# The bank of a gate product: from the transposes' pool of two to the w_in product's pool of three

## The chip, the cores and the metric
One core of a Trainium2 chip runs the program. The metric is the device time of one execution in microseconds (us), as a median over runs. The profile is one more execution, seen through the hardware profiler.

## What is computed
Two batches of 768 tokens go through three stages. The second and third are cut here to what matters:

```python
attn_out = _attn_ref(q, k, v)                 # linear attention with decay, 8 heads of 64
x = attn_out.transpose(0, 2, 1, 3).reshape(B, S, H * D)      # (2, 768, 512)
h = np.maximum(x @ w_in, 0.0)                 # w_in 512 x 1024
gate = 1 / (1 + np.exp(-conv3(h, conv_w)))    # over neighbouring tokens
x = (h * gate) @ w_out                        # w_out 1024 x 512
logits = x @ w_gate                           # 8 experts, and w_local beside it
h = np.maximum(x[b, s] @ w1[e], 0.0)          # e: the token's expert
out[b, s] = p[e] * (h @ w2[e])
```

The kernel doesn't wait for `x` to have the logits: it forms `w_out @ [w_gate, w_local]` (1024 x 9) once and multiplies it by `h * gate`.

## The kernel before
The order of instructions on each engine is the order in which the program's Python issues them; a scheduler only adds the waits. Several generators are advanced by hand, so that their steps interleave.

**The attention** goes over 48 chunks (8 pairs of heads, 6 chunks of 128 tokens). PSUM has eight banks: one for the gate's logits (`psl`), five for the attention (`ps1`: two for `s_ps`, one for `inc`, two for `y`), one for the conversions (`psg`), one for the w_in product (`psa`).

**The w_in product** of a batch is done in 8 blocks of 128 of the 1024 hidden columns (`ffn_in`). A block has two halves, a and b, of 384 tokens; each half is one PSUM tile `h_ps`, filled by four *slices* (k = 0 to 3) of three matmuls each (L133 to L135), and then evicted by ScalarE (L364). I count the slices of the first batch from 0, eight a block: slices 0 to 19 are issued in the attention's shadow, slice 20 (the second half of block 2) is the first behind it. `tick()` runs after each slice and issues the next step of the blocks already multiplied: L338 (ScalarE), L341 twice (VectorE), L343 (sigmoid, ScalarE), L345 (VectorE), L314 (ScalarE), L318 (VectorE), and in the end the gate's logits (`logit`, L332, TensorE), which need the block's gate weights `wc[:, m]`.

**The conversions** (`convert`) bring the weights, which come as 64-bit words, to two fp32 parts. A conversion loads its words (`raw`), narrows them (L149 and L150 VectorE, L151 ScalarE, L153 GpSimd, into a tile `na`), writes the high part (L171 ScalarE) and the low part (L173). For a block m of w_out it goes on: TensorE transposes the block (*turn m*, L182, tile `wt_ps`), ScalarE copies it to SBUF (L186, tile `wt` in the pool of `na`), TensorE multiplies it by the gate's weights (*product m*, L190, tile `wc_ps`, 9 columns), and ScalarE copies those into `wc` (*gate copy m*, L192). `advance()` moves all running conversions by one step, once per chunk and behind the attention once per slice. The list `turning` holds back a turn while as many blocks as `banks` has entries are between turn and gate copy.

Behind the attention the pools are made anew: `psa` has three banks, for `h_ps`, `psg` two and `psb` two (the w_out product's), and `banks` gets its second entry. Blocks 0 and 1 of w_out have then been turned, and product 1 is the first to be issued; seven products (1 to 7) and six turns (2 to 7) are left. In the kernel before both `wt_ps` and `wc_ps` come from `psg`:

```python
        ps = psg.tile([P, 4, P], F32, tag="g", name="wt_ps")     # L180, the turn's
        pg = psg.tile([P, E + 1], F32, tag="g", name="wc_ps")    # the product's
```

A new tile waits for the last reader of the tile that had its bank. Both kinds are read by ScalarE alone, and so is `h_ps`.

After that: the second batch's w_in product, the w_out product and the routing (L474 to L642), and then the experts (11 tiles of tokens and 2 of quarters), for which SyncE fetches weights in 152 transfers of 512 KB.

Of the kernel before, what the change touches and what calls it, by code (L numbers as in the profile page):

```python
# [9 lines left out]
F32 = mybir.dt.float32  # L10
# [11 lines left out]
E, F = 8, 1024  # L22
NT = B * S
P = 128
# [67 lines left out]
def tile_kernel(ctx, tc, cat, cst, qT, kT, kN, vN, w_in, conv_w, w_out, wg, w1, w2, out):  # L92
# [4 lines left out]
    def pool(name, bufs, stack=ctx, **kw):  # L97
        return stack.enter_context(tc.tile_pool(name=name, bufs=bufs, reuse_waits="tile", **kw))
# [17 lines left out]
    psg = pool("psg", 1, ps_stack, space=PSUM)  # L116
    psa = pool("psa", 1, ps_stack, space=PSUM)
# [23 lines left out]
    def raw_words(src, n):  # L141
        r = p1.tile([P, 512, 2], I32, tag="raw", name="raw", bufs=3)
        sy.dma_start(out=r[:, 0:n].rearrange("p n t -> p (n t)"), in_=src.bitcast(I32))
        return r[:, 0:n, 0], r[:, 0:n, 1]

    def narrow(words, n):
        lo, hi = words
        a = p1.tile([P, 512], I32, tag="na", name="na", bufs=4)[:, 0:n]
        ve.tensor_scalar(out=a, in0=hi, scalar1=3, scalar2=0x3FFFFFF8, op0=ALU.logical_shift_left, op1=ALU.bitwise_and)  # L149
        ve.scalar_tensor_tensor(out=a, in0=hi, scalar=-0x40000000, in1=a, op0=ALU.bitwise_and, op1=ALU.bitwise_or)  # L150
        se.activation(out=lo, in_=lo.bitcast(U32), func=AF.Copy, scale=2.0 ** -29)  # L151
        yield 2
        po.tensor_tensor(out=a, in0=a, in1=lo, op=ALU.add)  # L153
        yield 2
        return a.bitcast(F32)

    turning, held, loaded, ready, banks = [], [], [], [], [0]

    def convert(src, hi, lo, m=None):

        while len(loaded) > 2:
            yield 1
        loaded.append(src)
        words = raw_words(src, 512)
        yield 6
        while len(held) > 2:
            yield 1
        held.append(src)
        w = yield from narrow(words, 512)
        loaded.pop()  # L170
        se.activation(out=hi, in_=w, func=AF.Copy)  # L171
        yield 2
        (po if m is None else ve).tensor_tensor(out=lo, in0=w, in1=hi.bitcast(F32), op=ALU.subtract)  # L173
        if m is None:
            held.pop()
            return
        while len(turning) >= len(banks):
            yield 1
        turning.append(m)
        ps = psg.tile([P, 4, P], F32, tag="g", name="wt_ps")  # L180
        for k in range(4):
            te.transpose(ps[:, k, :], w[:, k * P:(k + 1) * P], ident)  # L182
        held.pop()
        yield 2
        wt = p1.tile([P, 512], F32, tag="na", name="wt", bufs=4).rearrange("p (k n) -> p k n", k=4)
        se.activation(out=wt, in_=ps, func=AF.Copy)  # L186
        yield 2 if len(banks) == 1 else 7
        pg = psg.tile([P, E + 1], F32, tag="g", name="wc_ps")
        for k in range(4):
            te.matmul(pg, wt[:, k, :], wgs[:, k, :], start=(k == 0), stop=(k == 3))  # L190
        yield 1
        se.activation(out=wc[:, m, 0:E + 1], in_=pg, func=AF.Copy)  # L192
        turning.remove(m)
        ready.append(m)
# [220 lines left out]
    for i in range(len(seq) + LOOK):  # L415
        if i < len(seq):
            p, c = seq[i]
            heads[p].scores(c)
            if c == 0 and p + 1 < 8:
                running.append([heads[p + 1].prepare(), 2])  # L420
            if i in STARTS:
                running.append([convert(*parts.pop(0)), 1])
            if i in LOADS:
                load(LOADS[i])
            if i == 14:
                running.append([small(), 1])
        todo = rest
        if i >= LOOK:
            p, c = seq[i - LOOK]
            rest = heads[p].output(c)  # L430
        if todo:
            todo()
        advance()
        while i >= FIRST and slices < (i - FIRST + 1) * RATE:
            next(first)
            slices += 1
# [6 lines left out]
    psa = pool("psa", 3, q_stack, space=PSUM)  # L443
    psg = pool("psg", 2, q_stack, space=PSUM)
# [330 lines left out]
    psa = pool("psc", 1, space=PSUM)  # L775
# [270 lines left out]
```

## Time and profile before
| | us |
|---|---|
| median of 3 runs | 443.0 |
| lowest, highest run | 442.42, 445.74 |
| the profiled execution | 441.8 |
| its span, first to last instruction | 440.0 |
| TensorE busy in it | 409.7 (93%) |
| VectorE, ScalarE, GpSimd busy | 289.3, 260.0, 91.7 |

The mean granted clock of TensorE is 0.984 of its full speed. All times that follow are from the start of the span. In the rows of the order of time a busy TensorE is modelled at its ends, so the start of the next instruction often lies before the end of the one ahead; distances are therefore taken from start to start where there are two.

### The profile page before, as it was taken

Reading aid. Unit: us, or ns where it says so; the run is one execution under the profiler, and the core shown is the slowest. Engines: PE = TensorE matmul, PEld = TensorE weight load, DVE = VectorE, ACT = ScalarE, POOL = GpSimd, SP = SyncE. Lnnn points to the kernel's source line nnn. Section 1 sums busy time; section 2 is a strip of 40 time slices with the busy share of each in tenths; the row PEclk is TensorE's granted clock in tenths of the full one; section 3 lists DMA queues with packets and bytes.
Section 4 is the critical chain, followed back from the end, with each engine's and each line's share of the span. In section 5 each row is a group of like instructions: output and inputs, shape, how many; then the busy total and the mean of one; then the engine's idle time right before and its main releaser. Section 6 shows DMA issues by size and latency. Waiting matters only on the chain.

```text
span 440.0 us, 7232 instructions
## 1 busy us (share of the span) xinstructions
PE 409.7 (93%) x2378; PEld 324.6 (74%) x2378; DVE 289.3 (66%) x517; ACT 260.0 (59%) x429; POOL 91.7 (21%) x93
## 2 busy tenths in 40 slices
PE   4988999986999999999899999999999999999992
PEld 3877988876888778988677775757767676777781
DVE  3798789677648270277789237747776876857750
ACT  3786776755666313566614147757777875866760
POOL 5366663221100000000000330032232123111210
PEclk9999999987999999999999999999999999999998
DMA  7989763310000011000097998899999998893001
GB/s 250 370 310 364 243 237 97 97 49 1 1 0 1 30 43 48 25 1 0 1 349 247 358 340 290 301 367 413 399 372 334 385 365 301 333 324 127 18 26 52
DMA packets 27324, 86.59 MB, mean 197 GB/s; under 512 B 3598, under 2 KB 4622, under 8 KB 27280
## 3 DMA queue, kind: packets, MB, share of 16 engines
q1 hardware_dynamic: 25200, 79.76, 50.0%
q0 software_dynamic: 2080, 6.29, 3.8%
q8 instruction: 21, 0.34, 0.3%
q14 instruction: 23, 0.19, 0.1%
HBM read 105.18 MB, written 6.55 MB: 254 GB/s over the span
## 4 chain that ended last, share of the span: by engine, by line
PE 33%; issue 25%; DMA 17%; DVE 16%; ACT 5%; POOL 1%; SPq 0%; POOLq 0%; DVEq 0%; ACTq 0%
DMA out_dram<-yo,it 15%; DVE cc L341 4%; PE x_ps L133 4%; PE h_ps L133 4%; PE y L288 3%; PE x_ps L134 3%; PE x_ps L135 3%; PE h_ps L134 3%; PE h_ps L135 3%; PE s_ps L270 3%; DVE cc L345 2%; PE inc L278 2%; DVE na L149 1%; ACT cc L343 1%; PE y L290 1%
## 5 line engine op out<-in xcount | busy, mean ns | idle before, releaser
L341 DVE SCALAR_TENSOR_TENSOR cc<-h,cw,cc 128x768 f32<-128x768 f32 x32 | 34.4, 1074 | 22.3 <-ACT cc L338 22.3
L133 PE MATMUL h_ps<-xT,wih 128*128 128x384 f32 x128 | 47.2, 369 | 0.0
L848 POOL DMA_INDIRECT out_dram<-yo,it x13 | 18.1, 1395 | 138.5 <-ACT yo L847 138.5
L712 POOL DMA_INDIRECT xg<-xs,it x13 | 17.3, 1334 | 126.7 <-DMA qc<-in_w_dram 119.3
L134 PE MATMUL h_ps<-xT,wih 128*128 128x384 f32 x128 | 43.7, 341 | 0.0
L135 PE MATMUL h_ps<-xT,wil 128*128 128x384 f32 x128 | 43.6, 340 | 0.0
L133 PE MATMUL x_ps<-woh,hg 128*128 128x512 f32 x96 | 38.6, 402 | 0.0
L134 PE MATMUL x_ps<-wol,hg 128*128 128x512 f32 x96 | 37.5, 391 | 0.0
L135 PE MATMUL x_ps<-woh,hg 128*128 128x512 f32 x96 | 37.4, 390 | 0.0
L703 DVE TENSOR_TENSOR wc<-r,wc 128x1024 fp32r<-128x1024 f32 x22 | 25.9, 1220 | 16.5 <-ACT wc L702 16.5
L270 PE MATMUL s_ps<-qz,kq 128*128 128x256 f32 x96 | 30.6, 405 | 5.6 <-DMA kq<-in_kT_dram 3.5
L703 DVE TENSOR_TENSOR ws0l<-r,ws0l 128x1024 fp32r<-128x1024 f32 x22 | 26.0, 1222 | 11.2 <-ACT ws0l L702 11.0
L703 DVE TENSOR_TENSOR ws1h<-r,ws1h 128x1024 fp32r<-128x1024 f32 x22 | 26.0, 1221 | 10.7 <-ACT ws1h L702 10.2
L288 PE MATMUL y<-at,vz 128*128 128x128 f32 x192 | 31.5, 287 | 1.2 <-DVE xT L293 0.6
L703 DVE TENSOR_TENSOR ws0h<-r,ws0h 128x1024 fp32r<-128x1024 f32 x22 | 26.0, 1222 | 8.6 <-ACT ws0h L702 8.4
L153 POOL TENSOR_TENSOR na<-na,raw 128x512 int32<-128x512 int32 (+1 forms) x17 | 21.9, 1288 | 41.0 <-DVE na L150 10.6
L702 ACT ACTIVATE ws0l<-r 128x1024 fp32r<-128x1024 f32 x22 | 22.1, 1052 | 13.1 <-PE y L135 13.1
L702 ACT ACTIVATE wc<-r 128x1024 fp32r<-128x1024 f32 x22 | 22.1, 1054 | 11.9 <-PE g L135 11.9
L288 PEld LDWEIGHTS y<-at,vz 128*128 128x128 f32 x192 | 26.2, 197 | 3.7 <-DVE xT L293 2.3
L272 DVE TENSOR_TENSOR at<-s_ps,ca 128x256 f32<-128x256 f32 x48 | 20.1, 420 | 11.8 <-PE s_ps L270 11.8
L133 PEld LDWEIGHTS h_ps<-xT,wih 128*128 128x128 f32 x128 | 24.6, 192 | 3.0 <-issue 2.1
L318 DVE TENSOR_TENSOR hg<-cc,hg 128x768 fp32r<-128x768 f32 x16 | 15.3, 958 | 16.3 <-ACT hg L314 16.3
(228 smaller groups left out, 1026.1 us busy)
## 6 DMA issues: line engine op xcount, KB each, us to landing
r<-in_w_dram SPq DMA_DIRECT2D x88, 512.0 KB
qc<-in_w_dram SPq DMA_DIRECT2D x32, 512.0 KB
qs1l<-in_w_dram SPq DMA_DIRECT2D x32, 512.0 KB
raw<-in_w_in_dram SPq DMA_DIRECT2D x8, 512.0 KB
raw<-in_w_out_dram SPq DMA_DIRECT2D x8, 512.0 KB
kq<-in_qT_dram SPq DMA_DIRECT2D x7, 384.0 KB
kq<-in_kT_dram SPq DMA_DIRECT2D x7, 384.0 KB
kv<-in_vN_dram SPq DMA_DIRECT2D x7, 384.0 KB
```

What stands on the lines that cost most here:

```text
L133: te.matmul(ps, lhi, rhi, start=first, stop=False)
L134: te.matmul(ps, lhi, rlo, start=False, stop=False)
L135: te.matmul(ps, llo, rhi, start=False, stop=last)
L153: po.tensor_tensor(out=a, in0=a, in1=lo, op=ALU.add)
L270: te.matmul(ps, self.kq[:, 0, tok], self.qz[:, :, tok], start=True, stop=True)
L272: ve.tensor_tensor(out=self.at[c], in0=ps, in1=self.dm, op=ALU.mult)
L288: te.matmul(y, vz[:, c, j, :], at[:, j, :], start=(j == 0), stop=(c == 0 and j == 1))
L341: ve.scalar_tensor_tensor(out=cc, in0=h[:, i:i + S], scalar=cw[:, m, i:i + 1], in1=cc, op0=ALU.mult, op1=ALU.add)
L702: se.activation(out=w[:, 0, h, :], in_=r, func=AF.Copy)
L703: ve.tensor_tensor(out=w[:, 1, h, :], in0=r, in1=w[:, 0, h, :].bitcast(F32), op=ALU.subtract)
L712: return po.indirect_dma_start(out=xg, out_offset=None, in_=xs[0:n], in_offset=bass.IndirectOffsetOnAxis(ap=it[:, j:j + 1], axis=0), bound ...
L848: po.indirect_dma_start(out=out, out_offset=bass.IndirectOffsetOnAxis(ap=it[:, j:j + 1], axis=0), in_=yo, in_offset=None, bounds_check=NT ...
```

## The change
One line of `convert`. While `banks` has one entry (during the attention) the product's tile still comes from `psg`, only with 512 columns of which 9 are used. Later it comes from `psa`, under the tag of `h_ps`, so that `psg` (two banks) is left to the turns, and `psa` (three banks) is shared by `h_ps` and `wc_ps`. The matmuls, their count and their order are the same.

```diff
         yield 2 if len(banks) == 1 else 7
-        pg = psg.tile([P, E + 1], F32, tag="g", name="wc_ps")
+        pg = (psg.tile([P, 512], F32, tag="g", name="wc_ps") if len(banks) == 1 else psa.tile([P, 512], F32, tag="a", name="wc_ps"))[:, 0:E + 1]
         for k in range(4):
             te.matmul(pg, wt[:, k, :], wgs[:, k, :], start=(k == 0), stop=(k == 3))
```

## Rows read from the trace of the kernel before
**Rows 1.** Long stretches: length, busy us per engine, PEclk, DMA share, GB/s.
```profile
115.00:215.00 100.00, 99.32 (x593) 85.28 (x592) 54.43 (x76) 49.88 (x77) 0.53 (x1) 1.00 0.04 17
215.00:275.00 60.00, 55.74 (x315) 42.01 (x314) 38.88 (x99) 25.11 (x34) 7.42 (x9) 1.00 0.81 291
275.00:430.00 155.00, 154.58 (x835) 108.05 (x834) 108.13 (x107) 108.14 (x143) 33.56 (x28) 1.00 0.78 290
```
**Rows 2.** TensorE's waits, 92 to 112 us: total us, times, longest.
```profile
PE wt_ps L182 <- ACT wc L192: 6.1, 2, 4.2
```
**Rows 3.** TensorE in order: start, length, line, tile [idle before, releaser].
```profile
32.65 0.46 PE L278 MATMUL inc<-kv 128*128 128x128 f32 x2 [1.56 <-DVE st L285]
...
95.33 1.09 PE L182 MATMUL wt_ps<-cs,na 128*128 128x128 f32 x4 [1.88 <-ACT wc L192]
...
98.65 0.44 PE L133 MATMUL h_ps<-xT,wih 128*128 128x384 f32 x1
...
101.88 0.95 PE L190 MATMUL wc_ps<-wgs,wt 128*128 128x9 f32 x8
...
103.30 0.95 PE L190 MATMUL wc_ps<-wgs,wt 128*128 128x9 f32 x8
108.47 1.08 PE L182 MATMUL wt_ps<-cs,na 128*128 128x128 f32 x4 [4.21 <-ACT wc L192]
...
111.85 0.42 PE L133 MATMUL h_ps<-xT,wih 128*128 128x384 f32 x1
...
114.03 0.34 PE L133 MATMUL h_ps<-xT,wih 128*128 128x384 f32 x1
...
126.72 0.95 PE L190 MATMUL wc_ps<-wgs,wt 128*128 128x9 f32 x8
```
**Rows 4.** ScalarE in order of time, 95 to 130 us.
```profile
95.56 0.69 ACT L151 ACTIVATE raw<-raw 128x512 int32<-128x512 uint32 x1
98.30 0.49 ACT L364 ACTIVATE h<-h_ps 128x384 f32<-128x384 f32 x1 [2.05 <-PE h_ps L135]
...
100.51 0.68 ACT L151 ACTIVATE raw<-raw 128x512 int32<-128x512 uint32 x1
101.08 0.63 ACT L171 ACTIVATE woh<-na 128x512 fp32r<-128x512 f32 x1
...
104.93 0.84 ACT L314 ACTIVATE hg<-cc 128x768 fp32r<-128x768 f32 x1 [2.84 <-DVE cc L345]
106.89 0.84 ACT L343 ACTIVATE cc<-cc 128x768 f32<-128x768 f32 x1 [1.12 <-DVE cc L341]
...
108.16 0.16 ACT L192 ACTIVATE wc<-wc_ps 128x9 f32<-128x9 f32 x1
...
129.46 0.17 ACT L192 ACTIVATE wc<-wc_ps 128x9 f32<-128x9 f32 x1
```
**Rows 5.** VectorE in order of time, 100 to 107 us.
```profile
100.66 1.02 DVE L341 SCALAR_TENSOR_TENSOR cc<-h,cw,cc 128x768 f32<-128x768 f32 x1 [3.81 <-ACT cc L338]
101.59 0.68 DVE L173 TENSOR_TENSOR wol<-na,woh 128x512 fp32r<-128x512 f32 x1
102.87 0.43 DVE L149 TENSOR_SCALAR na<-raw 128x512 int32<-128x512 int32 x1 [0.60 <-PE wc_ps L190]
...
104.81 2.05 DVE L341 SCALAR_TENSOR_TENSOR cc<-h,cw,cc 128x768 f32<-128x768 f32 x1
```
**Rows 6.** Short stretches, columns as in the first group; PEclk is the granted clock.
```profile
32.00:33.00 1.00, 0.35 (x3) 0.35 (x3) 0.95 (x5) 0.41 (x1) 1.00 (x1) 1.00 0.98 359
94.50:95.00 0.50, 0.00 (x0) 0.00 (x0) 0.50 (x1) 0.50 (x1) 0.00 (x0) 0.63 0.94 377
98.00:98.50 0.50, 0.50 (x10) 0.16 (x8) 0.00 (x0) 0.20 (x1) 0.40 (x1) 0.96 0.00 0
104.50:105.00 0.50, 0.00 (x0) 0.00 (x0) 0.50 (x2) 0.07 (x1) 0.50 (x1) 0.86 0.00 0
111.50:112.00 0.50, 0.50 (x5) 0.50 (x5) 0.00 (x0) 0.50 (x1) 0.00 (x0) 0.81 0.00 0
```

## The prediction
> **What bounds the kernel now.** I read first the busy time by long stretches [rows 1]: from 115 to 215 us TensorE works 99.32 of 100 us and from 275 to 430 us 154.58 of 155, and between them 55.74 of 60. Whatever TensorE is late by at 115 us it is therefore still late by at the end, unless something else holds those stretches; the change acts only before that, between the attention's last chunk (about 91 us) and the last gate product (about 128 us). The waits of TensorE in that stretch are one group [rows 2]: 6.1 us in two waits, both the turn of a w_out block (L182) waiting for a gate copy (L192). TensorE's instructions in order of time [rows 3] show them: turn 3 waits 1.88 us until 95.33, turn 4 waits 4.21 us until 108.47. ScalarE's order [rows 4] tells why the copies are late: gate copy 2 (108.16) stands behind L314 (104.93, waited 2.84) and L343 (106.89, waited 1.12), which wait for VectorE. VectorE in turn [rows 5] stood 3.81 us before L341 at 100.66, waiting for ScalarE's L338, and 0.60 us before L149 at 102.87, waiting for product 2 itself. ScalarE stood 2.05 us before the eviction at 98.30, because TensorE had been late with that half block. So the first wait helps to make the second.
>
> Both waits cost more than their length. The granted clock [rows 6] was 1.0 (2.4 GHz) until TensorE had stood still for 1.2 us (0.63 in the half microsecond from 94.5, so it fell to 0.5, 1.2 GHz, at about 94.63), and came back at about 98.02, 2.69 us after work began again. In the second wait it fell at about 104.86 and came back at about 111.69, 3.22 us after the restart at 108.47. Work in those stretches ran at half speed, so each lost about half: 1.35 and 1.61 us.
>
> **The change, part by part.** During the attention nothing moves: the tile is one bank as before and comes from the same pool of one. Its shape alone changes, which costs nothing, since the matmul still writes 9 columns. No instruction is added, removed or moved on any engine, and no DMA; every yield and the count of blocks being turned stay. What changes is which bank products 1 to 7 write, and so which eviction a tile waits for.
>
> *Removed:* a turn no longer waits for a gate copy. With two banks for turns alone, turn m waits for L186 of turn m-2. For turn 4 that copy ran long before (it is ahead of 98.30 on ScalarE). Turn 3 finds a bank free that the attention's last output has left. So the 1.88 us go, and the half-speed stretch behind it. From 95.33 to slice 24 at 98.65 are 3.32 us [rows 3], 2.69 of them at half speed; at full speed 1.98. Slice 24 starts at 93.45 + 1.98 = 95.43. The six slices to product 2 take 101.88 - 98.65 = 3.23, product 2 and slice 30 take 103.30 - 101.88 = 1.42, and the product's end is 108.47 - 4.21 - 103.30 = 0.96 later: turn 4 can start at 101.04. The 3.38 us from turn 4 to slice 32 (111.85) ran at half speed, so about 1.9 at full: TensorE would reach slice 32 at about 103.
>
> *Added:* in the pool of three banks an `h_ps` may now find a gate product in its bank, and a product an `h_ps`. A pool here gives a new tile the buffer that is freed first: L149 at 102.87 waits for product 2 [rows 5], whose input it replaces, although an older tile of the same pool was still held. All evictions of these banks are on ScalarE, so banks come free in ScalarE's order: copy 1, half block 2b, 3a, copy 2, 3b, copy 3, 4a. The fourth tile takes the first of these, and so on: 3b takes copy 1's bank, product 2 takes 2b's, product 3 takes 3a's, and 4a (slices 32 to 35) takes the bank of **copy 2**. That is the very copy for which turn 4 waited before. The wait is not removed, it goes from turn 4 to slice 32, behind a turn, a slice, a gate logit and another turn. Behind slice 32 on TensorE stands everything; behind its eviction stand L338 and the whole chain on ScalarE and VectorE.
>
> When does copy 2 come? ScalarE's eviction of 2b was late by TensorE alone. Without that it follows L151 (95.56), which takes 101.08 - 100.51 = 0.57 to the next start: 96.13 for 98.30, 2.17 earlier. L338 and L341 (100.66) follow back to back and move by 2.17, and so does L173 (101.59, 0.68 long) to 99.42. L149 then starts at its end, 100.10, for 102.87, as product 2 is done at 99.6: 2.77 earlier. L345, L341 (2.05 long, beside a GpSimd add that moves with it), L343 and copy 2 follow with the same distances. Copy 2: 108.16 - 2.77 = 105.39. TensorE restarted 0.31 behind its start (108.47 - 108.16): slice 32 at 105.70 for 111.85, **6.15 earlier**. The new wait is from about 103.0 to 105.70, 2.7 us.
>
> *The clock behind the new wait.* 1.88 us of waiting lost the clock; 1.56 us at 32.65 did not (granted 1.0 in that microsecond) [rows 3, 6]. 2.7 us is beyond both, so I take it as lost, for 2.69 to 3.22 us of work, at half speed: 1.35 to 1.61, say 1.48. The bounds are 0 (it holds) and twice that, 3.0 (a second slow stretch). The Trainium skill (TensorE: Matmul & The Clock Gate, HAM oscillation — how this bites in real kernels) holds only idle gaps beyond a bound against the clock, and both 1.88 and 2.7 lie under its bound; by that rule no clock is lost and the sum is 6.15. The row of 1.88 disagrees with it.
>
> The sum: 6.15 - 1.48 = **4.67 us**, reached at slice 36 (114.03 before). Behind it the banks are no limit by the same order of release: blocks 4 to 7 take banks whose eviction is four slices (114.03 - 111.85 = 2.18 us) or more old. The copy that is latest behind its product is number 7, 129.46 - 126.72 = 2.74 us [rows 3, 4]; its bank goes to the second half of block 7, nine slices behind, about 4.9 us. From 115 us on TensorE carries the gain [rows 1]; the 4.26 us in which it stands between 215 and 275 are waits on its own results and on work that they started, and move with it. The experts' weight transfers begin when the memory of `xT` is free, by the code, so they move too.
>
> Against its own time: 441.8 - 4.7 = 437.1 us, span 440.0 - 4.7 = 435.3. The runs shown have a median of 443.0, 1.2 above the profiled one; I predict for a like median: 443.0 - 4.7 = **438.3 us**.
>
> **The rivals.**
> *The clock holds in the new wait.* For it: 1.56 us did not lose it, and 2.7 is only 0.8 more than 1.88; against it: both longer waits here did. Gain 6.15, 436.9 us. Chance 0.15.
>
> *A bank in turn, or a longer slow stretch.* If banks were given round and round, 4a would take 3b's: slice 32 then waits for that eviction too, which is behind copy 2 and L151 (0.57) and takes 0.49, some 0.95 in all, and the second half of block 6 would wait for the eviction just before it, some 0.75. Gain 4.67 - 1.7 = 3.0, 440.0 us. Two slow stretches give 6.15 - 3.0 = 3.15, nearly the same. Against the first is the row of L149. Chance 0.15.
>
> *The chain does not move.* If VectorE's chain is bound by something that I took for ScalarE's lateness, copy 2 stays at 108.16, and slice 32 starts at 108.47, 3.38 earlier, with the same clock lost: gain 1.9, 441.1 us. For it: the copy depends on a dozen instructions of three engines, of which I followed only those on the longest path; against it: the waits of 3.81 and 2.05 us [rows 4, 5], which name who was late. Chance 0.10; that nothing at all is gained, 0.03.
>
> *Slower: the product's bank blocks `h_ps` in every pair.* Gate copies stand in ScalarE's queue behind instructions that wait for VectorE. If the pairs 4/5 and 6/7 also meet a wait of 2.7 and the clock behind it, 1.48, they cost 2 x 4.2 = 8.4 against 4.7: 446.7 us. It decides where a copy comes later behind its product than the bank's next tile, so where the 2.74 of product 7 grows past some 4.9. The Trainium skill (the same page, A second HAM failure mode: psum-queue depth-cycling) speaks for it: cycling through PSUM banks makes TensorE stand briefly and often, until the clock swings. In the kernel before no `h_ps` waits for its bank in this stretch [rows 2], so no row shows it. Chance 0.07.
>
> **How the numbers follow.** The forecast has 0.50, with a range of its own from 4.1 to 5.2 us of gain (the slow stretch, and 0.2 for the steps read from starts). A measurement of this kernel can tell about 1% from no change, 4.4 us. The forecast is beyond that in seven of ten, 0.35; with the held clock's 0.15 faster has 0.50. Within 1% has the forecast's other 0.15 and the three smaller gains, 0.28: 0.43. Slower 0.07. The range for eight in ten goes from the held clock, with 0.5 for the scatter of runs, 436.3, to the unmoved chain with as much, 441.6.
>
> **What would show it.** Right: no wait of L182 for L192; slice 24 near 95.4; L149 of block 6 near 100.1; one wait of TensorE of 2 to 3 us, of an L133, ended by L192, near 105.7; granted clock 0.5 behind it for about 3 us; slice 36 near 109.4. Wrong: L133 waiting for L364; the clock at 1.0 throughout; copy 2 still near 108; more than one `h_ps` wait before 130 us; or TensorE idle longer than 4.3 us between 215 and 275.

## The result, and the profile after

The median is 438.59 us (437.87 to 439.1) beside 444.13 us for the kernel before on the same chip: a ratio of 0.9875, 95% interval 0.9827 to 0.9922. The profiled execution took 438.87 us with a span of 437.1 and a mean granted clock of 0.989. Each engine issues its instructions in the same order as before.

TensorE's waits from 92 to 130 us in the kernel after: total us, times, longest. There is one, and it is no longer the turn (L182) that waits for a gate copy [rows 2], but the matmul that opens an `h_ps` tile.

```profile
PE h_ps L133 <- ACT wc L192: 2.3, 1, 2.3
```

TensorE in order of time, kernel after: start, length, line, tile, idle time before it and what ended it. The lines answer to [rows 3]: product 1, turn 3, slice 24, turn 4, slices 32 and 36.

```profile
92.32 0.95 PE L190 MATMUL wc_ps<-wgs,wt 128*128 128x9 f32 x8
...
94.14 0.60 PE L182 MATMUL wt_ps<-cs,na 128*128 128x128 f32 x4
...
96.19 0.45 PE L133 MATMUL h_ps<-xT,wih 128*128 128x384 f32 x1
...
101.69 0.64 PE L182 MATMUL wt_ps<-cs,na 128*128 128x128 f32 x4
...
106.34 0.44 PE L133 MATMUL h_ps<-xT,wih 128*128 128x384 f32 x1 [2.32 <-ACT wc L192]
...
109.98 0.45 PE L133 MATMUL h_ps<-xT,wih 128*128 128x384 f32 x1
```

Turns 3 and 4 wait for nothing. All the waiting of the stretch now stands before slice 32. Product 1 starts at 92.32 here and at 91.47 in the trace of before. The lag arises in the attention's first 14 us: TensorE stood 3.04 us for a transfer of `kq` there, until 8.62, where it had gone on at 7.64. (That alone is not the reason: `again` has a like wait, until 8.50, and starts product 1 at 91.55.) So 0.85 us are taken off these times when they are set against the prediction.

ScalarE in order of time, kernel after (answers to [rows 4]): the eviction of 2b, the two instructions that wait for VectorE, gate copy 2, and the eviction of 3b behind it.

```profile
96.96 0.48 ACT L364 ACTIVATE h<-h_ps 128x384 f32<-128x384 f32 x1
...
102.89 0.85 ACT L314 ACTIVATE hg<-cc 128x768 fp32r<-128x768 f32 x1 [2.16 <-DVE cc L345]
104.86 0.84 ACT L343 ACTIVATE cc<-cc 128x768 f32<-128x768 f32 x1 [1.12 <-DVE cc L341]
...
106.13 0.16 ACT L192 ACTIVATE wc<-wc_ps 128x9 f32<-128x9 f32 x1
...
106.75 0.48 ACT L364 ACTIVATE h<-h_ps 128x384 f32<-128x384 f32 x1
```

VectorE in order of time, kernel after (answers to [rows 5]). L149 of block 6 has lost its wait for product 2, and the wait of L341 is 1.63 us for 3.81.

```profile
99.30 1.02 DVE L341 SCALAR_TENSOR_TENSOR cc<-h,cw,cc 128x768 f32<-128x768 f32 x1 [1.63 <-ACT cc L338]
100.23 0.68 DVE L173 TENSOR_TENSOR wol<-na,woh 128x512 fp32r<-128x512 f32 x1
100.84 0.42 DVE L149 TENSOR_SCALAR na<-raw 128x512 int32<-128x512 int32 x1
...
101.90 0.95 DVE L345 TENSOR_TENSOR cc<-cc,h 128x768 f32<-128x768 f32 x1
102.77 2.06 DVE L341 SCALAR_TENSOR_TENSOR cc<-h,cw,cc 128x768 f32<-128x768 f32 x1
```

Stretches of the kernel after: length, busy us (instructions) of PE, PEld, DVE, ACT and POOL, granted clock, DMA share, GB/s (answers to [rows 1, 6]).

```profile
106.50:107.00 0.50, 0.50 (x3) 0.50 (x4) 0.47 (x2) 0.50 (x2) 0.00 (x0) 0.80 0.00 0
110.00:110.50 0.50, 0.50 (x4) 0.50 (x3) 0.50 (x1) 0.28 (x1) 0.00 (x0) 0.79 0.00 0
115.00:215.00 100.00, 97.94 (x582) 83.30 (x583) 55.00 (x76) 49.84 (x75) 0.53 (x1) 1.00 0.04 17
215.00:275.00 60.00, 57.26 (x317) 43.47 (x319) 40.12 (x100) 26.20 (x37) 7.39 (x9) 1.00 0.85 306
275.00:430.00 155.00, 152.47 (x820) 106.26 (x812) 104.01 (x103) 105.03 (x138) 33.53 (x28) 1.00 0.76 284
```

One slow stretch is left, and it begins behind the wait: the clock fell to 0.5 at about 106.8 (a half microsecond at 0.80 is 0.3 at full speed and 0.2 at half), 0.46 us after slice 32 had started, and came back at about 110.2. Slices 32 to 36 took 3.64 us. TensorE stands 2.06 us in the first of the long stretches and 2.74 in the second, together 4.80, where it had stood 0.68 and 4.26 [rows 1], together 4.94: one wait has moved over the border at 215 with the rest. In the third stretch it is at work, but for 0.4 us, until its last product ends, at 427.9.

### The profile page after: what moved, and what is told of

The parts are those of the page before. It is cut to its first block, busy times and chain, and to the rows that moved or that the text cites. A ratio compares the mean times of both kernels' runs of the same rounds, so it can differ in the third digit from the quotient of the medians.

```text
span 437.1 us, 7229 instructions
## 1 busy us (share of the span) xinstructions
PE 409.0 (94%) x2378; PEld 324.2 (74%) x2378; DVE 290.1 (66%) x517; ACT 259.9 (59%) x429; POOL 91.6 (21%) x93
## 4 chain that ended last, share of the span: by engine, by line
PE 31%; issue 26%; DMA 17%; DVE 17%; ACT 5%; POOL 1%; SPq 1%; POOLq 0%; DVEq 0%; ACTq 0%
DMA out_dram<-yo,it 16%; DVE cc L341 4%; PE x_ps L133 4%; PE y L288 3%; PE x_ps L135 3%; PE x_ps L134 3%; PE h_ps L133 3%; PE s_ps L270 3%; PE h_ps L135 3%; PE h_ps L134 3%; DVE cc L345 2%; PE inc L278 2%; DVE na L149 2%; ACT cc L338 1%; ACT cc L343 1%
## 5 line engine op out<-in xcount | busy, mean ns | idle before, releaser
L133 PE MATMUL h_ps<-xT,wih 128*128 128x384 f32 x128 | 47.2, 369 | 2.3 <-ACT wc L192 2.3
L341 DVE SCALAR_TENSOR_TENSOR cc<-h,cw,cc 128x768 f32<-128x768 f32 x32 | 35.1, 1096 | 18.0 <-ACT cc L338 17.9
L133 PE MATMUL x_ps<-woh,hg 128*128 128x512 f32 x96 | 38.6, 402 | 0.0
L153 POOL TENSOR_TENSOR na<-na,raw 128x512 int32<-128x512 int32 (+1 forms) x17 | 21.9, 1291 | 38.7 <-ACT raw L151 13.0
L133 PEld LDWEIGHTS h_ps<-xT,wih 128*128 128x128 f32 x128 | 24.7, 193 | 5.5 <-ACT wc L192 2.6
L702 ACT ACTIVATE ws1h<-r 128x1024 fp32r<-128x1024 f32 x22 | 22.1, 1053 | 6.6 <-PE g L135 6.3
```

The source lines that it names most:

```text
L133: te.matmul(ps, lhi, rhi, start=first, stop=False)
L341: ve.scalar_tensor_tensor(out=cc, in0=h[:, i:i + S], scalar=cw[:, m, i:i + 1], in1=cc, op0=ALU.mult, op1=ALU.add)
L702: se.activation(out=w[:, 0, h, :], in_=r, func=AF.Copy)
```

## The experiments

**A measure without the scatter of the ends.** The median of the kernel before lay between 442.85 and 444.13 us from one set of runs to the next, and stages outside the change differ between executions: from the routing's last L517 to the experts' first L877 it was 42.3 to 45.4 us in the fourteen profiles. So beside the median I read from each profile the stretch from the start of product 1 to the start of the routing's first matmul (L517): it holds all that the change touches. One profile each.

| kernel | stretch, us | less than before | median, us | ratio to before, 95% |
|---|---|---|---|---|
| before | 62.09 | | 443.0 | |
| after | 57.31 | 4.78 | 438.59 | 0.9875 (0.9827 to 0.9922) |
| again | 56.25 | 5.84 | 437.99 | 0.9899 (0.9875 to 0.9923) |
| after3 | 57.34 | 4.75 | 437.95 | 0.9891 (0.9847 to 0.9936) |
| first_only | 59.86 | 2.23 | 440.58 | 0.9957 (0.9938 to 0.9976) |
| rest_only | 59.37 | 2.72 | 441.56 | 0.9973 (0.9945 to 1.0002) |
| own_banks | 59.18 | 2.91 | 439.24 | 0.9919 (0.9893 to 0.9946) |
| later | 54.20 | 7.89 | 434.6 | 0.984 (0.9795 to 0.9885) |
| later_again | 54.24 | 7.85 | 436.59 | 0.9852 (0.9815 to 0.989) |
| later_old | 56.90 | 5.19 | 437.28 | 0.9871 (0.9842 to 0.99) |
| later_own | 55.28 | 6.81 | 435.11 | 0.982 (0.9779 to 0.986) |
| keep_busy | 56.25 | 5.84 | 438.0 | 0.9892 (0.9858 to 0.9925) |
| fill_old | 61.21 | 0.88 | 444.27 | 1.002 (0.9995 to 1.0045) |
| fill_rest | 58.94 | 3.15 | 440.58 | 0.9924 (0.9892 to 0.9956) |

In kernels with inserted lines the numbers behind them are shifted: by 2 in `later`, `later_again`, `later_old` and `later_own` (L192 is L194), by 4 in `fill_old` and `fill_rest` (L192 is L196), and by 4 from L359 on in `keep_busy`.

### The change once more, twice
No edit: the kernel after.

> The changed kernel once more, in more rounds, since about 1% is in question. The theory (both waits of a turn for a gate copy go, a shorter wait of an h_ps for the same copy comes, and the rest of the kernel carries the difference): 4.7 us less than before, ratio 0.9895, and in the profile again one wait of L133 for L192 of 2 to 3 us. If the first runs' 5.5 us (ratio 0.9875) were the true size, some 0.8 us would come from a place that the theory does not have.

> The kernel after once more, beside the two below on one chip. 0.99 of before; the 2.32 us stand ahead of slice 32 in each execution, with a slow stretch behind it in some executions and none in others.

TensorE in order of time, `again`.

```profile
105.60 0.44 PE L133 MATMUL h_ps<-xT,wih 128*128 128x384 f32 x1 [2.32 <-ACT wc L192]
```

A stretch of it, columns as above; the last but two is the granted clock.

```profile
106.50:107.00 0.50, 0.50 (x5) 0.50 (x4) 0.50 (x2) 0.50 (x2) 0.12 (x1) 1.00 0.00 0
```

The wait is the same to the hundredth, and the clock stays at 1.0. In `after3`, behind the same wait, it fell again:

```profile
106.50:107.00 0.50, 0.50 (x4) 0.50 (x4) 0.47 (x2) 0.50 (x2) 0.00 (x0) 0.85 0.00 0
```

Slices 32 to 36 take 2.19 us in `again` and 3.64 in the kernel after: the slow stretch costs 1.45 us there, of which the routing's start sees 57.31 - 56.25 = 1.06. So the same kernel has two outcomes behind one wait, and neither is "the" price. The medians are 4.9 us below before in both sets of runs (4.5 and 4.8 by the ratios), where 4.7 was expected and the first runs had 5.5.

### Product 1 alone, and the others alone
The lines with a minus, here and in the next group, are those of the kernel after, and dots stand for the rest of a line.

```diff
-        pg = (psg.tile(...) if len(banks) == 1 else psa.tile(...))[:, 0:E + 1]
+        pg = (psa.tile(...) if m == 1 else psg.tile(...))[:, 0:E + 1]     # first_only
+        pg = (psa.tile(...) if m > 1 else psg.tile(...))[:, 0:E + 1]      # rest_only
```

> Only product 1 takes its bank from the pool of the w_in product, products 2 to 7 are as before. The theory: the first wait and its slow stretch go, turn 4 still waits for copy 2, which comes 2.8 us earlier since the chain on ScalarE and VectorE moves, and loses the clock as before: 2.8 us less than before, ratio 0.9937. The rival that the chain does not move: turn 4 starts at 108.47 as before, and nothing is gained (ratio 1.0). The rival that all of the gain is the first wait and its slow stretch: 4.5 to 5 us less.

> Product 1 keeps its bank in the pool of the turns, products 2 to 7 take theirs from the pool of the w_in product. The theory: turn 3 waits 1.9 us as before, and with it the chain is as late as before; turn 4 does not wait, slice 32 waits for copy 2 and starts at about 108.5 instead of 111.85, loses the clock behind it, and slice 36 is 1.9 us earlier: 1.9 us less, ratio 0.9957; together with first_only about the whole 4.7. The rival that the gain is one wait only: 0 or 4.7.

TensorE in order of time, `first_only`.

```profile
105.75 1.09 PE L182 MATMUL wt_ps<-cs,na 128*128 128x128 f32 x4 [4.65 <-ACT wc L192]
```

The same of `rest_only`.

```profile
95.63 0.63 PE L182 MATMUL wt_ps<-cs,na 128*128 128x128 f32 x4 [1.89 <-ACT wc L192]
...
108.95 0.44 PE L133 MATMUL h_ps<-xT,wih 128*128 128x384 f32 x1 [2.07 <-ACT wc L192]
```

Each half takes away its own wait and leaves the other. With product 1 alone moved, turn 3 runs through, and the second wait comes sooner and is longer: 4.65 us until 105.75 for 4.21 until 108.47 [rows 3]. Copy 2 comes at 105.44 for 108.16, so the first wait does help to make the second. With the others moved, turn 3 still waits 1.89 us, and the second wait stands before slice 32, at 108.95 for 111.85. The stretches gain 2.23 and 2.72, together 4.95, about what the whole change gains (4.78). By the ratios both gain less than was expected (1.9 for 2.8 and 1.2 for 1.9 us), together 3.1, where the whole change gains 4.5 in the same set of runs (`again`); the intervals, of 0.8 to 1.3 us to either side, don't tell these apart.

### The products in the third pool
That is `psb`, the w_out product's pool of two.

```diff
-  ... else psa.tile([P, 512], F32, tag="a", name="wc_ps"))[:, 0:E + 1]
+  ... else psb.tile([P, 512], F32, tag="x2", name="wc_ps"))[:, 0:E + 1]
```

> The products behind the attention take their bank from the w_out product's pool of two, which is idle in this stretch: neither a turn nor an h_ps can wait for a gate copy. The theory that the chain on ScalarE and VectorE, not the bank, sets the pace: slice 32 starts at about 103 without a wait, and TensorE then stands some 2 to 3 us before the gate's logit of block 2 (L332), for L345, which comes no earlier than with the change; the clock falls there; within 0.5 us of the changed kernel, 4.5 to 5.2 us less than before. The rival that the bank is what limits: the wait of 2.3 us and the slow stretch of 1.5 go, 3 to 4 us less than the changed kernel, 8 us less than before, ratio 0.982.

No `h_ps` waits any more, yet the kernel is no faster than the kernel after: 1.25 us behind `again` by the median, and the rival's much larger gain is not there. TensorE in order of time, `own_banks`: the gate logit of block 2.

```profile
110.31 0.53 PE L332 MATMUL lg<-cc,wc 128*32 128x192 f32 x8 [2.74 <-DVE cc L345]
```

The same logit in `again`, behind the wait for the bank:

```profile
110.15 0.53 PE L332 MATMUL lg<-cc,wc 128*32 128x192 f32 x8
```

Two stretches of `own_banks`, where the clock fell and where it came back.

```profile
112.00:112.50 0.50, 0.50 (x6) 0.50 (x4) 0.50 (x1) 0.36 (x1) 0.00 (x0) 0.90 0.00 0
119.00:119.50 0.50, 0.50 (x4) 0.50 (x4) 0.00 (x0) 0.50 (x2) 0.00 (x0) 0.77 0.00 0
```

The wait has moved on to the gate's logit, whose operand VectorE's L345 makes in the same chain. Counted from product 1 the logit starts at 18.65 us here and at 18.60 in `again`: without the wait for the bank TensorE comes no further. The slow stretch behind it, from about 112.4 to 119.2, is 6.8 us long. The bank tells where TensorE stands; the chain of ScalarE and VectorE tells how late it is.

### The chain made shorter, with and without the change
Two conversions later: blocks 6 and 7 of w_out are narrowed only when four blocks are ready, so that L149 and L150 of block 6 no longer stand in VectorE's queue ahead of the L345 of block 1 (the "second block" of the expectations, since they start at 0). ScalarE's L151 and L171 and GpSimd's L153 of block 6 move back with them.

```diff
-        while len(held) > 2:
+        while len(held) > 2 or (m is not None and m > 5 and len(ready) < 4):
             yield 1
+        if m == 7:
+            yield 8
         held.append(src)
```

> The kernel after, with the conversions of blocks 6 and 7 of w_out held back until the second block's feed-forward part has its activations, so that L149 and L150 of block 6 no longer stand in VectorE's queue ahead of the L345 of the second block. Theory (with the wait on banks gone, the chain of ScalarE and VectorE from the gate to copy 2 on L192 sets when slice 32 starts): about 1.06 us of VectorE leaves the chain ahead of L345, the L341 that takes 2.05 us beside a GpSimd addition becomes about 1 us shorter, an L171 leaves ScalarE ahead of copy 2 (0.5 us). Copy 2 some 2.6 us earlier than in the kernel after, slice 32's wait of 2.32 us at most 0.5 us, the second gate logit with hardly a wait, the clock at 1.0. Time 2.5 to 3 us less than the kernel after, about 7 us less than before, ratio about 0.9835. Rival (TensorE's own work or the banks set the pace there, and the chain is hidden): no difference from the kernel after, ratio about 0.990.

> The kernel before (the change undone), with the same holding back of the conversions of blocks 6 and 7. Theory: the first wait on a bank (about 1.9 us at the third turn, with the clock's loss behind it) stays, as the conversions it waits for are untouched; copy 2 comes some 3 us earlier and the second wait shrinks with it. About 3.3 us less than before, ratio about 0.9926, and so some 4 us behind the same edit on the kernel after. Rival (the two edits take away the same wait): the same time as that edit on the kernel after, ratio about 0.984.

> The kernel after with the conversions of blocks 6 and 7 held back, once more, for a direct comparison. Theory (the chain of ScalarE and VectorE to copy 2 sets slice 32 in the kernel after): 2.5 to 3.4 us less than the kernel after of this call, ratio to before 0.983 or 0.984. Rival (its lead in the call before was scatter): within 1 us of the kernel after.

VectorE in order of time, `later`: the multiplication of block 1 by its gate (L345 in the kernel after), the second multiply-add of block 2 behind it (L341 there), and one of block 3.

```profile
100.22 0.95 DVE L347 TENSOR_TENSOR cc<-cc,h 128x768 f32<-128x768 f32 x1
101.09 1.01 DVE L343 SCALAR_TENSOR_TENSOR cc<-h,cw,cc 128x768 f32<-128x768 f32 x1
...
104.91 2.10 DVE L343 SCALAR_TENSOR_TENSOR cc<-h,cw,cc 128x768 f32<-128x768 f32 x1 [0.27 <-ACT cc L340]
```

ScalarE there: the sigmoid of block 2 and gate copy 2.

```profile
102.14 0.85 ACT L345 ACTIVATE cc<-cc 128x768 f32<-128x768 f32 x1
102.89 0.16 ACT L194 ACTIVATE wc<-wc_ps 128x9 f32<-128x9 f32 x1
```

TensorE there: slice 32 and the gate logit of block 2 (the "second" of the expectations).

```profile
103.10 0.44 PE L133 MATMUL h_ps<-xT,wih 128*128 128x384 f32 x1
...
107.93 0.53 PE L334 MATMUL lg<-cc,wc 128*32 128x192 f32 x8 [0.40 <-DVE cc L347]
```

What was expected of the chain is there: VectorE's multiplication starts at 100.22 for 101.90, the next instruction takes 1.01 us for 2.06, copy 2 comes at 102.89 for 106.13, and slice 32 starts at 103.10 without a wait. Counted from product 1 (91.67 here, 92.32 in the kernel after) copy 2 is 2.6 us earlier, as expected. The slow form of 2.10 us is still there, but behind copy 2. From 90 to 130 us the clock stays at 1.0, in `later_again` too. The stretch is 3.1 us shorter than in the kernel after, 2.0 shorter than in `again`. Beside runs of the kernel after on the same chip the median is 1.4 us less (436.59 and 437.95); by the ratios of both sets of runs it is some 2 us, less than the 2.5 to 3 expected, and the intervals overlap. The two profiles have the same stretch (54.20 and 54.24), but the span of `later_again` is 2.3 us longer, and its trace shows where: TensorE waited for a gather of the experts' tokens, and the clock fell to 0.5 behind it, until about 249.5.

```profile
245.35 1.35 PE L800 MATMUL tp<-cs,xg 128*128 128x128 f32 x8 [2.08 <-DMA xg<-xs,it]
```

```profile
246.00:246.50 0.50, 0.50 (x6) 0.50 (x5) 0.00 (x0) 0.00 (x0) 0.00 (x0) 0.61 1.15 115
```

With the change undone (`later_old`), TensorE in order of time:

```profile
95.39 0.63 PE L184 MATMUL wt_ps<-cs,na 128*128 128x128 f32 x4 [1.85 <-ACT wc L194]
...
106.33 0.63 PE L184 MATMUL wt_ps<-cs,na 128*128 128x128 f32 x4 [0.28 <-ACT wc L194]
```

A stretch of it behind the first wait:

```profile
96.50:97.00 0.50, 0.50 (x4) 0.38 (x2) 0.41 (x1) 0.00 (x0) 0.00 (x0) 0.58 0.00 0
```

The first wait stays and the second all but goes, as the theory had it, but the gain is 5.7 us by the ratio (5.19 on the stretch) where 3.3 were expected. The expectation counted the wait alone and forgot the slow stretch that goes with it, 1.61 us by the prediction's own sum: 3.3 + 1.6 = 4.9. The rival, that both edits take away the same wait, holds for the second wait alone: with the change the stretch is 2.7 us shorter still (54.20 for 56.90). By their times the two are not told apart, since the intervals overlap.

### Both together
`later` with the products in the third pool (the edits above).

> The same holding back, with the products' banks from the third pool, the one that the gate logits and the feed-forward sums use, in place of the pool of the w_in product. With the conversions in place this choice moved the stand from slice 32 to the second gate logit (2.74 us). Theory (that stand was the wait for VectorE's L345 in the same chain, which the holding back brings 2.5 us forward): the logit's wait 0.5 us or less, no slow stretch, the time of the holding back on the kernel after within 1 us, ratio 0.984. Rival (the pool itself is short by one bank with the products in it): a stand of 2 us or more stays on a tile of that pool, ratio about 0.990.

TensorE in order of time, `later_own`.

```profile
107.84 0.53 PE L334 MATMUL lg<-cc,wc 128*32 128x192 f32 x8 [0.63 <-DVE cc L347]
```

A stretch of it, where the clock fell.

```profile
110.50:111.00 0.50, 0.50 (x6) 0.50 (x6) 0.47 (x2) 0.50 (x2) 0.00 (x0) 0.93 0.00 0
```

The wait of the logit fell from 2.74 to 0.63, so it was the chain's (0.5 or less was expected). But here the clock fell at about 110.9 with no wait of a microsecond ahead of it, which was not expected. The times of `later`, `later_again` and `later_own` are not told apart; the medians of all three are below the kernel after, and they are the lowest found.

### TensorE kept at work where it stands
Matmuls of 128x512 into a bank that nobody reads: ten ahead of slice 32 of the kernel after (`keep_busy`), seven ahead of turn 3 of the kernel before (`fill_old`) and of `rest_only` (`fill_rest`). They are extra work that the result doesn't use.

```diff
+        if m == 3:
+            fill = psb.tile([P, DM], F32, tag="x2", name="fill")
+            for _ in range(7):
+                te.matmul(fill, wi_hi[:, 0, 0:P], wi_hi[:, 0, 0:512], start=True, stop=True)
         ps = psg.tile([P, 4, P], F32, tag="g", name="wt_ps")
```

> The kernel after, with ten matmuls of 128x512 of one loaded tile with itself into a bank that nobody reads, just ahead of slice 32, where TensorE stands 2.32 us. Theory (the stand is what lets the clock fall in those executions that lose it): the granted clock stays 1.0 from 92 to 116 us, slice 32 starts at the same time as in the kernel after, and the mean over executions is about 0.7 us less than the kernel after (some half of them lose about 1.4 us), ratio about 0.988. Rival 1 (the clock falls from something else): a stretch at 0.5 stays, same time as the kernel after, 0.990. Rival 2 (the ten matmuls themselves overrun copy 2 and hold slice 32 up): slice 32 later by what they exceed the wait, up to 0.5 us, ratio about 0.991.

> The kernel before, with seven matmuls of 128x512 (about 1.8 us by the 2.54 us that ten took) into a bank that nobody reads, just ahead of the third turn, where TensorE stands 1.88 us. In three profiled kernels with this stand the clock fell to 0.5 behind it. Theory (the stand is what lets the clock fall): it stays at 1.0 there, turn 3 starts when it did, and the stretch from the third turn to the second stand is some 1 us shorter by its matmuls at the full clock; but the second stand waits for a chain of ScalarE and VectorE, which takes part of that back. The first L517 stands 61 to 62.1 us behind the first product, where it was 62.1 before; the time 0 to 1.1 us less than before, ratio 0.9975 to 1.0. Rival (the clock falls from something else, the work between the attention and the turns): 0.5 behind the seven matmuls as before, time as before or up to 0.3 us more.

> The same seven matmuls ahead of the third turn, on the kernel in which only the products behind the first take a bank of the other pool (its stand ahead of the third turn was 1.89 us, with the clock at 0.5 for some 3.5 us behind it). Theory: the clock stays at 1.0 behind the third turn; some 1 us less from the first product to the first L517 (59.4 us there), where the chain lets it; ratio about 0.995 where it was 0.997. Rival: the slow stretch stays, ratio 0.997 or above.

TensorE in order of time, `fill_old`: the extra matmuls and turn 3.

```profile
93.50 1.79 PE L183 MATMUL fill<-wih 128*128 128x512 f32 x7
95.55 0.63 PE L186 MATMUL wt_ps<-cs,na 128*128 128x128 f32 x4 [0.26 <-ACT wc L196]
```

A stretch of it, behind turn 3.

```profile
96.00:98.00 2.00, 2.00 (x18) 1.45 (x17) 1.03 (x3) 1.22 (x3) 0.68 (x1) 1.00 0.05 10
```

TensorE in order of time, `fill_rest`: turn 3 and slice 32.

```profile
95.49 0.63 PE L186 MATMUL wt_ps<-cs,na 128*128 128x128 f32 x4 [0.27 <-ACT wc L196]
...
107.30 0.44 PE L133 MATMUL h_ps<-xT,wih 128*128 128x384 f32 x1 [2.07 <-ACT wc L196]
```

Two stretches of it, behind turn 3 and behind slice 32.

```profile
96.00:98.00 2.00, 2.00 (x18) 1.45 (x17) 0.98 (x2) 1.20 (x3) 0.73 (x1) 1.00 0.04 8
108.50:109.00 0.50, 0.50 (x4) 0.50 (x3) 0.42 (x1) 0.50 (x1) 0.42 (x1) 0.76 0.00 0
```

The same place in `rest_only`, without the matmuls:

```profile
96.50:97.00 0.50, 0.50 (x5) 0.49 (x3) 0.50 (x1) 0.04 (x1) 0.00 (x0) 0.96 0.00 0
```

Without the matmuls the clock fell in or behind this wait in all three profiles that have it (`before`, `rest_only`, `later_old`: at 94.63, about 96.96 and about 96.58); with them it stayed at 1.0 in both. So, as far as five profiles tell, the stand is what loses it there. The stretch gets 0.88 and 0.43 us shorter, the second with a new slow stretch behind the wait of 2.07 us, which had kept the clock in `rest_only`. The ratio of `fill_rest` is 0.9924, where `rest_only` had 0.9973 and 0.995 was expected; their intervals overlap. In the time of `fill_old` nothing of it is seen (1.002). Its profile tells where the gain went in that execution. TensorE's waits from 250 to 275 us, in `fill_old` and in the kernel before (L789 is L785 there), name a gather of the experts' tokens, which the edit doesn't touch. First `fill_old`, and a stretch of it behind that wait:

```profile
PE tp L789 <- DMA xg<-xs,it: 2.0, 1, 2.0
```

```profile
261.50:262.00 0.50, 0.50 (x3) 0.50 (x4) 0.00 (x0) 0.00 (x0) 0.00 (x0) 0.67 0.99 402
```

And the kernel before:

```profile
PE tp L785 <- DMA xg<-xs,it: 0.9, 1, 0.9
```

The gather came later, and behind it the clock was at 0.5 until about 265.1, where the kernel before kept 1.0. From the routing's first matmul to the end of TensorE's last product `fill_old` takes 2.5 us more than the kernel before (280.7 and 278.2).

`keep_busy` kept the clock too, but so did `again` without the matmuls, and the two have the same stretch, 56.25, and the same median: that run settles nothing.

## Why the prediction was right, point by point

**The first wait goes.** As predicted: slice 24 at 96.19 - 0.85 = 95.34 (predicted 95.43), turn 4 at 100.84 (101.04), and no wait of L182. `first_only` shows this half by itself.

**The second wait moves to slice 32.** The order in which banks come free was read right: the wait is an L133's, ended by L192, the copy that had held turn 4. Slice 32 starts at 105.49 (105.70), after 2.32 us (2.7). The wait is shorter at both ends: its end by 0.21 us, and its start because the step there from turn 4 took 2.33 us (101.69 to 104.02), put at about 1.9 (1.77 by the prediction's own rows, with 3.22 of 3.38 us at half speed). `rest_only` shows that it is the later products' banks that move it.

**Copy 2 comes earlier by ScalarE's and VectorE's own chain.** L149 at 99.99 (100.10) and copy 2 at 105.28 (105.39). `later` and `own_banks` show that this chain, and not the bank, sets the time. The rival in which copy 2 stays at 108.16 fell, and so did the one of banks in turn: slice 32 started 0.21 us after copy 2 and waited for no eviction.

**The clock.** The loss of 1.48 us was sized right for the profiled execution (1.45), in part by luck: the prediction counted the slow stretch from the start of work, 2.69 to 3.22 us, but here the clock fell only behind that start, and the stretch of 3.4 us was not over at slice 36. (By the row of 0.96 [rows 6] the first return was at 98.04, not 98.02, which changes nothing.) But the step treated as one outcome what is two: behind the same wait of 2.32 us the clock fell in two of three profiles and held in the third, where the stretch gained 5.84 us. The rival "the clock holds" (6.15), given 0.15, is thus true in some executions; the gains by the medians, 5.5, 4.9 and 4.9 us, lie between the two. The row of 1.88 us [rows 3, 6] was no threshold. The Trainium skill (TensorE: Matmul & The Clock Gate, HAM oscillation — how this bites in real kernels) holds idle gaps against the clock only beyond a bound, and 1.88 and 2.32 both lie under it; by that rule neither loses the clock. The wait of 1.88 did, and that of 2.32 did in two of three profiles.

**The sum.** Slice 36 came 4.90 us earlier (4.67 predicted), and the stretch is 4.78 shorter. That the median of 438.59 lies so near to 438.3 is partly luck: the kernel before alone scatters by 1.3 us between sets of runs, and the forecast held for one of two outcomes of the clock.

**The gain is carried to the end.** It was, nearly to the last product. In the raw times the routing's first matmul is 153.56 - 149.63 = 3.93 earlier, which is the 4.78 less the late start of 0.85. The 4.26 us of standing were carried too (4.80 for 4.94 from 115 to 275). The span is 2.9 shorter, for 0.83 more went at the last eviction, ScalarE in order of time, kernel before:

```profile
432.17 0.69 ACT L847 ACTIVATE yo<-y,pr 128x512 f32<-128x512 f32 x1 [5.04 <-PEq L998]
```

And the kernel after:

```profile
429.12 0.69 ACT L847 ACTIVATE yo<-y,pr 128x512 f32<-128x512 f32 x1 [5.87 <-PEq L998]
```

That eviction waits for TensorE's queue 5.87 us where it waited 5.04. Why, no run here tells. By the medians of the first runs the gain is 444.13 - 438.59 = 5.5 us, and against the median shown before 443.0 - 438.59 = 4.4: the sum lies between.

**The slower rival.** No second `h_ps` waits for its bank before 130 us, so the pairs 4/5 and 6/7 cost nothing. For the rule of psum-queue depth-cycling (the Trainium skill, the same page, A second HAM failure mode: psum-queue depth-cycling) no run here shows a case: with seven products cycling through three banks the clock fell once at most between 90 and 130 us.

## What to carry to other kernels

A tile moved to another pool doesn't lose its wait; it hands it to whoever takes its bank next, so write down the order in which banks come free and name that tile. Then ask what makes the awaited instruction late: moving the bank won 4.8 us on the stretch, and taking two VectorE instructions out of the queue ahead of it won two to three more, and 5.2 by itself, with the bank left where it was. Price a stand of an engine with the slow clock behind it, as a chance and not as a rule, and a wait that goes takes both along.

## What was not expected of the hardware

The granted clock does not follow the length of a stand alone. It fell behind waits of 1.85, 1.88 and 1.89 us and held through one of 2.07 and one of 2.32, while other executions lost it behind the same 2.07 and 2.32; in `later_own` it fell some 3 us after a wait of 0.63. At the gathers it fell behind 2.00 (`fill_old`) and 2.08 us (`later_again`) and held through 2.63 (`keep_busy`). In the kernel before it fell while TensorE stood; in the kernel after 0.46 us after work had begun again. From fall to return the slow stretches between 90 and 130 us lasted 3.4 us in seven cases (the kernel after is one) and 6.8 in four (`own_banks`, `first_only`, and the second wait of the kernel before and of `fill_old`). What decides it stays open.

One VectorE form has no fixed length. GpSimd in order of time, kernel after:

```profile
102.21 1.79 POOL L153 TENSOR_TENSOR na<-na,raw 128x512 int32<-128x512 int32 x1 [2.97 <-DVE na L150]
```

There L341 took 1.01 us alone, 1.71 where a GpSimd addition (L153) that had begun before it ran on beside it for 0.89 us, and 2.06 where this one did so for 1.23 us, which the chain to copy 2 pays for in full. The L345 at 101.90 had begun 0.31 us ahead of that addition and kept its 0.95 us; the addition took 1.79 us, where two others of that trace took 1.29.
